# Keys' weight in four pieces between single tiles of x, and a new order for a linear-attention block with an MLP

## The chip, the cores and the metric

The kernel runs on one core of a Trainium2 chip. The time is that of one execution in microseconds of the device, from the chip's own clock; times of a profile are counted from the span's start.

## The reference

`x` is 2048 rows of 512 values in bf16. It is normalised row by row, goes through a linear attention of 32 heads of 16, is normalised again and goes through an MLP with ReLU and 1792 inner values; both parts are added to their input.

```python
h   = x + A(layernorm(x), wqkv, wo)
out = h + B(layernorm(h), w1, w2)

def A(x, wqkv, wo):
    q, k, v = heads(x @ wqkv)
    phi = lambda t: where(t > 0, t + 1, exp(t)) + 1e-6
    pq, pk = phi(q), phi(k)
    kv  = einsum("bhsd,bhse->bhde", pk, v)
    z   = sum of pk over the rows
    num = einsum("bhqd,bhde->bhqe", pq, kv)
    den = einsum("bhqd,bhd->bhq", pq, z) + 1e-6
    return (num / den) @ wo

def B(x, w1, w2):
    return maximum(x @ w1, 0) @ w2
```

## The kernel before

The 2048 rows are 16 tiles of 128 rows (0 to 15), and four chunks of four tiles each. Every instruction is put in its place by hand: `ORDER` is a text of words such as `K.1.3.0.2`, a name and its numbers. The kernel walks through the words and calls `op_<name>` with the numbers. Each engine executes its own instructions in this sequence; semaphores for the data are added automatically. No scheduler moves anything.

The words, by the engine that works on them:

- SyncE's queue (DMAs): `lx.t.n` loads n tiles of x from tile t on (L213); `lk`, `lq`, `lv`, `lo`, `l1`, `l2` load pieces k to k+n of a weight's 128-row blocks (`load_d`, L219); `X.t` and `x.t` transpose a normalised tile by DMA into `lnT` (L293, L294); `wb.c` writes the reciprocal denominators of a chunk to DRAM (L453) and `rb.c.h`, eight of them, read them back spread out into `rr` (L456); `fd.t` writes an output tile (L537). ScalarE's queue has `ax.t.n`, a load of x issued from there (L216).
- VectorE: `S.t` statistics (L233) and `A.t` mean and variance (L234) of a tile; `N.t` its normalised values (L247), by halves with `N.t.k.n`; `M` and `D` the minimum and the sum that finish phi of the keys (L326, L329), `qM`, `qD` of the queries; `dm` the product of queries and `rr` (L469); `hD`, `s`, `a`, `n` the same steps for the second normalisation; `pD` the MLP's ReLU (L513); `fo.t` the output tile (L530). The output tiles have four buffers; tile t uses number t modulo 4.
- ScalarE: `R.t.n` turns variances into 1/sqrt, as a Ln and an Exp (L239, L240); `E.t` copies transposed values from PSUM to `lnT` (L282); `F`, `U` the Exp and the ReLU of the keys (L319, L322), `qF`, `qU` of the queries; `dl4`, `dx4` the reciprocal of the denominators.
- TensorE: `warm` matmuls on zeros (L230); `T.t.b` transposes of a tile into bank b (L272), four of 128x128; `K.t.b` the keys of a tile, four matmuls (L301), by halves with two numbers more; `Q.c.j.b` queries of a chunk (L309); `G.t` the product of normalised x and phi of the keys, summed over all tiles (L353); `z` the sum of the keys (L377), `d4.c` the denominators of a chunk (L425), `kv` (L399) and `m` (L411) the small matrices; `h.t` attention's output (L478); `ph`, `p` the first and `f.t` the second layer of the MLP (L502, L493, L522; an `f` of a tile has 14 matmuls).

Tiles 0 to 4 are transposed by TensorE, tiles 5 to 15 by DMA. Which rows belong to a tile follows from the load words: a load of n tiles gives each partition n rows in a row.

Of the kernel before, what the change touches and what calls it, by code (L numbers as in the profile page):

```python
# [15 lines left out]


ORDER = """
ax.1.1 ax.2.1 table const masks warm.70.7.64 warm.2.7 lx.0.1 S.0 A.0 S.1 lk.0.4 R.0.1 N.0.0.2 lx.3.1 A.1 S.2
R.1.1 lx.4.2 T.0.3.0.2 N.0.2.2 A.2 E.0.0.2 R.2.1 T.0.2.2.2 E.0.2.2 lx.6.2 N.1 lq.0.4 K.0.5.0.2 T.1.3 S.3 lx.8.4  # L20
K.0.5.2.2 N.2 E.1 A.3 R.3.1 lx.12.4 T.2.6 E.2 S.5 N.3 S.4 K.1.0.0.2 A.5 F.0.1 K.1.0.2.2 T.3.3 E.3 K.2.2.0.2
K.2.2.2.2 A.4 S.7 K.3.3.0.2 Q.0.3.1 R.4.2 U.0.1 F.1.1 S.6 F.2.1 N.4 T.4.6 K.3.3.2.2 A.6 A.7 R.6.2 N.5 M.1.1
M.0.1 Q.0.1.5 Q.0.0.4 E.4 U.3.1 S.10 N.6 N.7 M.2.1 D.0.1 A.10 U.1.1 D.1.1 X.5 F.3.1 U.2.1 S.9 S.12 K.4.6 S.8
K.5.7 M.3.1 A.12 A.8 A.9 S.13 S.11 qU.0.0.2 X.6 qF.0.0.2 Q.0.2.0 D.2.1 A.11 K.6.2 A.13 X.7 U.4.2 F.4.2 R.8.2
qM.0.0.2 D.3.1 K.7.3 N.9 M.4.2 N.8 D.4.2 S.14 R.12.2 R.10.2 N.13 A.14 S.15 qF.0.2.2 X.9 N.10 A.15 G.0 G.2 G.1
N.12 G.3 G.4 G.5 X.8 F.6.2 U.6.2 X.13 K.9.3 R.14.2 qU.0.2.2 K.8.2 N.11 M.6.2 qD.0.0.2 D.6.2 N.15 N.14 F.8.2
U.8.2 K.13.1 X.12 X.11 qM.0.2.2 K.12.0 za.4.1 M.8.2 F.12.2 U.12.2 X.10 qD.0.2.2 G.7 K.11.3 X.14 K.10.2 G.6 D.8.2
za.6.0 X.15 K.14.0 F.10.2 M.12.2 lv.2.2 U.10.2 K.15.1 za.8.0 M.10.2 G.9 lv.0.2 zf D.10.2 G.8 zhi D.12.2 F.14.2
G.10 M.14.2 zlo G.12 U.14.2 D.14.2 z.3.3 z.0.3 z.1.3 z.2.3 zc zh G.14 d4.0.3 G.11 G.15 G.13 dl4.0 dx4.0 lo.0.2
gA.0.2 Q.1.1.3 Q.1.0.2 qF.1.0.2 lo.2.2 gD.2.2 kv.1.7 kv.2.7 kv.3.7 kv.0.7 qU.1.0.2 Q.1.3.1 qM.1.0.2 kx qD.1.0.2  # L30
Q.1.2.0 l1.0.2 m.3.7 m.2.6 mD.2.2 wb.0 rb.0.7 rb.0.3 rb.0.0 rb.0.6 rb.0.4 qF.1.2.2 qU.1.2.2 qM.1.2.2 Q.2.1.5
m.1.3 m.0.2 mA.0.2 rb.0.1 rb.0.2 Q.2.0.4 Q.2.3.1 Q.2.2.0 qF.2.0.2 qU.2.0.2 qD.1.2.2 rb.0.5 dm.0.2.2 dm.0.0.2
h.1.6 l1.2.2 d4.1.5 qF.2.2.2 qM.2.0.2 h.0.4 hD.1 dl4.1 s.1 dx4.1 a.1 hD.0 nA.1 s.0 a.0 n.0 Q.3.0.2 l2.0.7 h.2.5
hD.2 s.2 qU.2.2.2 Q.3.1.3 qU.3.0.2 wb.1 x.1 h.3.7 a.2 Q.3.3.6 hD.3 qF.3.0.2 n.2 Q.3.2.5 t.2.0 x.0 ph.0.3.1.0 s.3
a.3 n.3 ph.0.1.3.0 t.3.7 ph.0.0.2.0 rb.1.1 v.2 qM.2.2.2 r.0.4 rb.1.2 rb.1.5 qF.3.2.2 v.3 qM.3.0.2 qM.3.2.2
ph.0.2.0.0 ph.0.2.0.1 rb.1.7 ph.0.3.1.1 qD.2.0.2 qD.3.0.2 ph.0.0.2.1 qU.3.2.2 qD.3.2.2 qD.2.2.2 ph.0.1.3.1
p.0.9.5 p.0.8.4 pA.0.2.2 rb.1.3 rb.1.4 rb.1.6 d4.2.6.2 rb.1.0 dm.1.0.2 l2.7.7 dm.1.2.2 h.4.1 pD.0.0.2 dl4.2
dl4.3 dx4.2 wb.2 rb.2.6 hD.4 s.4 h.5.6 h.7.7 rb.2.7 hD.5 h.6.0 a.4 rb.2.0 rb.2.3 rb.2.4 pA.0.8.2 hD.7 hD.6 s.5
s.6 p.0.7.6 a.5 rb.2.1 p.0.6.5 p.0.4.2 p.0.5.3 s.7 a.6 a.7 p.0.13.1 rb.2.2 rb.2.5 n.4 n.7 n.5 n.6 pD.0.4.2
pD.0.6.2 p.0.11.4 p.0.12.0 dm.2.2.2 dm.2.0.2 dx4.3 p.0.10.3 pD.0.10.2 pD.0.12.2 wb.3 rb.3.4 f.2.6.0.7 rb.3.0  # L40
h.10.5 hD.10 x.6 h.9.4 hD.9 rb.3.2 rb.3.7 h.8.2 s.10 hD.8 a.10 h.11.0 s.9 s.8 rb.3.1 rb.3.6 rb.3.5 rb.3.3 hD.11
a.9 a.8 s.11 n.8 a.11 n.9 f.2.6.7.7 x.7 f.1.7.0.7 f.0.2.0.7 f.0.2.7.7 dm.3.0.2 n.10 n.11 dm.3.2.2 fo.2 fo.0
h.15.3 hD.15 x.5 x.4 x.11 h.12.4 h.13.0 s.15 hD.12 h.14.2 hD.13 a.15 s.12 f.3.3.0.7 x.10 r.4.4 p.1.0.1 hD.14
a.12 s.13 x.9 r.8.4 f.3.3.7.7 s.14 a.13 a.14 p.1.11.6 n.13 n.14 n.15 p.1.10.5 x.8 n.12 fo.3 pD.1.10.2 p.1.1.2
pD.1.0.2 f.1.7.7.7 fd.3 r.12.4 fo.1 p.1.6.3 fd.1 x.14 fd.2 p.1.7.4 p.1.3.1 p.1.4.6 p.1.5.7 p.1.2.0 pD.1.6.2
p.1.13.3 p.1.12.2 pD.1.4.2 pD.1.2.2 x.15 fd.0 x.12 pD.1.12.2 p.2.8.5 p.2.9.6 p.2.6.3 p.2.7.4 p.1.8.1 p.1.9.2
pD.2.8.2 pD.2.6.2 p.2.10.4 p.2.11.5 pD.1.8.2 pD.2.10.2 f.7.6.0.7 f.7.6.7.7 fo.7 p.2.0.4 p.2.1.5 f.4.0.0.7
f.4.0.7.7 x.13 pD.2.0.2 fo.4 f.6.1.0.7 fd.7 f.6.1.7.7 fo.6 f.5.3.0.7 f.5.3.7.7 p.3.4.5 p.3.5.6 fo.5 p.3.11.4
p.3.10.3 p.3.9.1 p.3.8.0 pD.3.4.2 p.3.6.5 p.3.7.6 pD.3.10.2 pD.3.8.2 pD.3.6.2 p.3.0.2 p.3.1.3 pD.3.0.2 p.3.3.1
p.3.2.0 pD.3.2.2 p.3.12.5 p.3.13.6 fd.4 fd.6 p.2.5.3 pD.3.12.2 f.15.4.0.14.3.1 fo.15.3.1 f.15.5.0.14.0.2  # L50
fo.15.0.2 fd.5 p.2.4.2 pD.2.4.2 p.2.3.1 p.2.2.0 p.2.12.6 pD.2.2.2 p.2.13.7 pD.2.12.2 f.8.1.0.7 f.8.1.7.7 fo.8
fd.8 f.12.4.0.7 f.12.4.7.7 fo.12 f.10.7.0.7 f.10.7.7.7 fo.10 f.13.6.0.7 fd.12 fd.10 fd.15.0.2 f.13.6.7.7 fo.13
fd.15.3.1 f.11.0.0.7 f.11.0.7.7 fo.11 fd.13 fd.11 f.14.3.0.7 f.14.3.7.7 fo.14 fd.14 f.9.0.0.7 f.9.0.7.7 fo.9
fd.9 f.15.6.0.14.2.1 fo.15.2.1 fd.15.2.1
"""


# [1 line left out]
def kernel(  # L59
# [157 lines left out]

    def load_d(dst, src, k, n):
        nc.sync.dma_start(out=dst[:, k : k + n, :], in_=src[:, k : k + n, :])  # L219
# [353 lines left out]
```

## Time and profile before

| | |
|---|---|
| median of 3 runs | 169.65 us (169.29 to 170.04) |
| the profiled execution: time / span | 169.61 / 167.9 us |
| granted TensorE clock | 1.00 |
| busy: TensorE / VectorE / ScalarE | 162.2 / 115.8 / 49.9 us |
| read from HBM / written | 9.96 / 2.62 MB |

Busy times are sums of an engine's instructions over the span. A matmul's record begins when its data enter and overlaps its neighbours, so a matmul of 512 columns has a record of 379 ns while the next follows 216 ns later; the chain of waits counts the latter. The profile's SPq and ACTq are the queues of DMA issues of SyncE and ScalarE; an issue's duration there is that of the issuing, and the landing is counted from the issue's start. L numbers are lines of the kernel before.

### The profile page before, as it was taken

Reading aid. Unit: us, or ns where it says so; the run is one execution under the profiler, and the core shown is the slowest. Engines: PE = TensorE matmul, PEld = TensorE weight load, DVE = VectorE, ACT = ScalarE, POOL = GpSimd, SP = SyncE. Lnnn points to the kernel's source line nnn. Section 1 sums busy time; section 2 is a strip of 40 time slices with the busy share of each in tenths; the row PEclk is TensorE's granted clock in tenths of the full one; section 3 lists DMA queues with packets and bytes.
Section 4 is the critical chain, followed back from the end, with each engine's and each line's share of the span. In section 5 each row is a group of like instructions: output and inputs, shape, how many; then the busy total and the mean of one; then the engine's idle time right before and its main releaser. Section 6 shows DMA issues by size and latency. Waiting matters only on the chain.

```text
span 167.9 us, 2399 instructions
## 1 busy us (share of the span) xinstructions
PE 162.2 (97%) x908; PEld 79.5 (47%) x924; DVE 115.8 (69%) x218; ACT 49.9 (30%) x84; POOL 4.7 (3%) x21
## 2 busy tenths in 40 slices
...
GB/s 147 372 234 96 18 106 95 186 315 37 131 341 157 106 228 72 147 43 118 106 94 31 31 89 132 2 0 31 31 66 0 0 0 0 0 66 55 31 62 39
DMA packets 25003, 16.01 MB, mean 95 GB/s; under 512 B 15008, under 2 KB 23968, under 8 KB 24992
## 3 DMA queue, kind: packets, MB, share of 16 engines
...
q8 instruction: 7, 0.11, 0.3%
...
HBM read 9.96 MB, written 2.62 MB: 75 GB/s over the span
## 4 chain that ended last, share of the span: by engine, by line
PE 93%; DVE 2%; DMA 2%; issue 1%
PE bk L522 29%; PE bk L493 26%; PE bk L478 8%; PE bk L301 8%; PE bk L353 8%; PE bk L309 8%; PE bk L502 2%; DMA x_nat<-in_A_x_dram 2%; DVE st L233 1%; PE bk L272 1%; PE bk L425 1%; DVE gT L530 1%; PE bk L377 1%; PE bk L399 1%; PE bk L411 1%
## 5 line engine op out<-in xcount | busy, mean ns | idle before, releaser
L522 PE MATMUL bk<-w_sb,at 128*128 128x512 bf16 (+2 forms) x250 | 49.8, 355 | 0.2
L493 PE MATMUL bk<-lnT,w_sb 128*128 128x512 bf16 x200 | 45.5, 379 | 0.3
L513 DVE TENSOR_SCALAR at<-bk 128x1024 bf16<-128x1024 f32 x26 | 31.4, 1222 | 11.8 <-PE bk L493 9.4
L522 PEld LDWEIGHTS <-at 128*128 128x128 bf16 x252 | 23.6, 98 | 25.4
L493 PEld LDWEIGHTS <-w_sb 128*128 128x128 bf16 x208 | 20.3, 98 | 24.1
L530 DVE SCALAR_TENSOR_TENSOR gT<-bk,rstd,h_nat 128x512 bf16<-128x512 f32 (+2 forms) x18 | 12.4, 691 | 25.5 <-PE bk L522 25.2
L319 ACT ACTIVATE eb<-bk 128x1024 bf16<-128x1024 f32 (+1 forms) x18 | 16.6, 937 | 4.3 <-PE bk L309 1.8
L322 ACT ACTIVATE rb<-bk 128x1024 bf16<-128x1024 f32 (+1 forms) x18 | 16.5, 933 | 0.6 <-PE bk L309 0.6
L301 PE MATMUL bk<-wk_sb,lnT 128*128 128x512 bf16 x62 | 15.4, 380 | 0.1
L309 PE MATMUL bk<-lnT,wq_sb 128*128 128x512 bf16 x62 | 15.3, 379 | 0.1
L478 PE MATMUL bk<-m_sb,pqs 128*128 128x512 bf16 x64 | 15.0, 379 | 0.0
L353 PE MATMUL bk<-at,h_nat 128*128 128x512 bf16 x55 | 13.0, 379 | 0.1
L239 ACT ACTIVATE rstd<-mv,eps 128x2 f32<-128x2 f32 (+2 forms) x14 | 4.2, 298 | 27.1 <-DVE mv L236 24.6
L233 DVE BATCH_NORM_STATS2 st<-x_nat 128x6 f32<-128x512 bf16 x16 | 10.5, 676 | 2.4 <-DMA x_nat<-in_A_x_dram 2.4
L484 DVE TENSOR_TENSOR h_nat<-bk,x_nat 128x512 bf16<-128x512 f32 x16 | 10.7, 679 | 1.0 <-PE bk L478 0.9
L235 DVE BATCH_NORM_STATS2 st<-h_nat 128x6 f32<-128x512 bf16 x16 | 10.6, 680 | 0.2
L478 PEld LDWEIGHTS <-pqs 128*128 128x128 bf16 x64 | 6.1, 98 | 7.8 <-issue 0.7
L309 PEld LDWEIGHTS <-wq_sb 128*128 128x128 bf16 x64 | 6.2, 98 | 7.3
L353 PEld LDWEIGHTS <-h_nat 128*128 128x128 bf16 x64 | 6.1, 98 | 7.3 <-issue 0.2
L301 PEld LDWEIGHTS <-lnT 128*128 128x128 bf16 x64 | 5.8, 98 | 6.8 <-DMA lnT<-h_nat 0.6
L326 DVE TENSOR_SCALAR eb<-eb 128x1024 bf16<-128x1024 bf16 (+1 forms) x18 | 6.8, 388 | 1.6 <-ACT eb L319 1.6
L247 DVE TENSOR_SCALAR h_nat<-x_nat,mv,rstd 128x512 bf16<-128x512 bf16 (+1 forms) x17 | 6.5, 396 | 0.2
...
## 6 DMA issues: line engine op xcount, KB each, us to landing
...
out_dram<-gT SPq DMA_DIRECT2D x15, 128.0 KB, 1.9
...
```

The lines of the kernel that those rows point to most:

```text
L233: op_S = lambda t: nc.vector.bn_stats(out=st[:, t, :], in_=x_nat[:, t, :])
L301: nc.tensor.matmul(bk[:, b, :], lhsT=lnT[c][:, kd, j * P : (j + 1) * P], rhs=wk_sb[:, kd, :], start=(kd == 0), stop=(kd == KD - 1),)
L309: nc.tensor.matmul(bk[:, b, :], lhsT=wq_sb[:, kd, j * P : (j + 1) * P], rhs=lnT[c][:, kd, :], start=(kd == 0), stop=(kd == KD - 1),)
L319: nc.scalar.activation(out=buf(eb, kind, i, n), in_=bank(at_bank[kind, i], n), func=ACT.Exp)
L322: nc.scalar.activation(out=buf(rb, kind, i, n), in_=bank(at_bank[kind, i], n), func=ACT.Relu)
L353: nc.tensor.matmul(bk[:, KD + kd, :], lhsT=ln_nat[:, t, kd * P : (kd + 1) * P], rhs=pk(t)[:, 0, :], start=(not stated), stop=(len(stated) ...
L478: nc.tensor.matmul(bk[:, b, :], lhsT=pqs[:, (c * KD + jb) % NQ, j * P : (j + 1) * P], rhs=m_sb[:, jb, :], start=(jb == 0), stop=(jb == KD ...
L484: nc.vector.tensor_tensor(out=h_nat[:, t : t + n, :], in0=bank(at_bank["h", t], n), in1=x_nat[:, t : t + n, :], op=ALU.add,)
L493: nc.tensor.matmul(bk[:, b, :], lhsT=w1_sb[:, kd, f * P : (f + 1) * P], rhs=lnT[c][:, kd, :], start=(kd == 0), stop=(kd == KD - 1),)
L513: nc.vector.tensor_scalar(out=acts[c % 2][:, f : f + n, :], in0=bank(at_bank["p", c, f], n), scalar1=-1.0, scalar2=0.0, op0=ALU.mult, op1= ...
L522: nc.tensor.matmul(bk[:, b, 0 : w * P], lhsT=acts[c % 2][:, f, j * P : (j + 1) * P], rhs=w2_sb[:, f, k * P : (k + w) * P], start=(f == 0), ...
L530: nc.vector.scalar_tensor_tensor(out=o_t[:, t % NO, cols], in0=bk[:, at_bank["f", t, k], 0 : w * P], scalar=rstd2[:, t : t + 1], in1=h_nat ...
```

## The change

- The keys' weight `wk` (512 KB) comes in four loads of 128 KB, one per 128-row block, between loads of single tiles of x, where it was one load.
- Tiles 1 and 2 are loaded from SyncE's queue, not from ScalarE's; every load is now issued by SyncE.
- Tile 0 is normalised, transposed and copied whole (`N.0`, `T.0.2`, `E.0`), and its keys are one `K.0.6`; they were done in two halves each.
- Tiles 8 to 15 come in one load (`lx.8.8`, 1 MB) instead of two of 4 tiles.
- The rest of `ORDER` is laid out anew, with other banks and another sequence; the set of matmuls is the same. A new function `op_ak` (a load of `wk` from ScalarE's queue) is defined and not used.

The diff, cut to the head of the order and the places that the prediction speaks of:

```diff
 ORDER = """
-ax.1.1 ax.2.1 table const masks warm.70.7.64 warm.2.7 lx.0.1 S.0 A.0 S.1 lk.0.4 R.0.1 N.0.0.2 lx.3.1 A.1 S.2
-R.1.1 lx.4.2 T.0.3.0.2 N.0.2.2 A.2 E.0.0.2 R.2.1 T.0.2.2.2 E.0.2.2 lx.6.2 N.1 lq.0.4 K.0.5.0.2 T.1.3 S.3 lx.8.4
-K.0.5.2.2 N.2 E.1 A.3 R.3.1 lx.12.4 T.2.6 E.2 S.5 N.3 S.4 K.1.0.0.2 A.5 F.0.1 K.1.0.2.2 T.3.3 E.3 K.2.2.0.2
-K.2.2.2.2 A.4 S.7 K.3.3.0.2 Q.0.3.1 R.4.2 U.0.1 F.1.1 S.6 F.2.1 N.4 T.4.6 K.3.3.2.2 A.6 A.7 R.6.2 N.5 M.1.1
...
-G.10 M.14.2 zlo G.12 U.14.2 D.14.2 z.3.3 z.0.3 z.1.3 z.2.3 zc zh G.14 d4.0.3 G.11 G.15 G.13 dl4.0 dx4.0 lo.0.2
-gA.0.2 Q.1.1.3 Q.1.0.2 qF.1.0.2 lo.2.2 gD.2.2 kv.1.7 kv.2.7 kv.3.7 kv.0.7 qU.1.0.2 Q.1.3.1 qM.1.0.2 kx qD.1.0.2
...
+table const masks warm.70.7.64 warm.2.7 lx.0.1 S.0 lx.1.1 lx.2.1 A.0 R.0.1 S.1 A.1 N.0 lk.0.1 S.2 lk.1.1 lk.2.1
+T.0.2 R.1.1 lx.3.1 N.1 T.1.7 E.0 A.2 lk.3.1 R.2.1 S.3 K.0.6 N.2 T.2.2 A.3 E.1 K.1.3.0.2 K.1.3.2.2 lx.4.2 S.5
+R.3.1 N.3 S.4 A.5 E.2 F.0.1 T.3.4 E.3 A.4 lx.6.2 S.7 S.6 K.2.7.0.2 K.2.7.2.2 lq.0.4 R.4.2 N.4 K.3.0.0.2 Q.0.3.1
+N.5 A.7 U.0.1 A.6 F.1.1 U.1.1 T.4.2 R.6.2 M.1.1 K.3.0.2.2 E.4 U.2.1 Q.0.0.3 M.0.1 U.3.1 D.1.1 lx.8.8 N.6 N.7
+D.0.1 X.5 Q.0.1.4 S.12 S.9 S.8 A.12 A.9 A.8 F.3.1 M.3.1 S.10 S.13 S.11 X.6 A.13 D.3.1 qF.0.0.2 qU.0.0.2 K.4.5
...
+K.14.0 K.15.1 za.8.0 zf F.14.2 lo.0.2 U.14.2 D.12.2 lo.2.2 M.10.2 G.9 l1.0.2 Q.1.1.3 zhi D.10.2 zlo M.14.2 G.11
+G.10 D.14.2 z.0.0 z.2.0 z.3.0 z.1.0 G.14 zc zh d4.0.0 dl4.0 dx4.0 wb.0 rb.0.2 G.13 rb.0.5 G.12 G.15 gA.2.2
...
+qD.1.2.2 dm.0.0.2 Q.2.2.0 Q.2.3.1 dm.0.2.2 h.1.2 qF.2.0.2 qU.2.0.2 l1.2.2 qM.2.0.2 qU.2.2.2 hD.1 d4.1.4 dl4.1
...
+p.0.11.7 dm.1.0.2 dm.1.2.2 h.6.1 pD.0.10.2 dl4.2 dx4.2 ph.0.0.2.1 hD.6 h.5.4 l2.7.7 pD.0.0.2 wb.2 rb.2.4 hD.5
...
+fo.12 fd.12 fd.13 fd.10 f.8.6.0.7 f.8.6.7.7 fo.8 fd.8 f.15.5.0.14.3.1 fo.15.3.1 fd.15.3.1
 """
...
+    def op_ak(k, n):
+        nc.scalar.dma_start(out=wk_sb[:, k : k + n, :], in_=wqkv_v[:, k : k + n, D : 2 * D])
+
     op_lk = lambda k, n: load_d(wk_sb, wqkv_v[:, :, D : 2 * D], k, n)
```

More of the change, by code (lines that the diff above doesn't have):

```diff
@@ L18 @@
 ORDER = """
-ax.1.1 ax.2.1 table const masks warm.70.7.64 warm.2.7 lx.0.1 S.0 A.0 S.1 lk.0.4 R.0.1 N.0.0.2 lx.3.1 A.1 S.2
-R.1.1 lx.4.2 T.0.3.0.2 N.0.2.2 A.2 E.0.0.2 R.2.1 T.0.2.2.2 E.0.2.2 lx.6.2 N.1 lq.0.4 K.0.5.0.2 T.1.3 S.3 lx.8.4
-K.0.5.2.2 N.2 E.1 A.3 R.3.1 lx.12.4 T.2.6 E.2 S.5 N.3 S.4 K.1.0.0.2 A.5 F.0.1 K.1.0.2.2 T.3.3 E.3 K.2.2.0.2
-K.2.2.2.2 A.4 S.7 K.3.3.0.2 Q.0.3.1 R.4.2 U.0.1 F.1.1 S.6 F.2.1 N.4 T.4.6 K.3.3.2.2 A.6 A.7 R.6.2 N.5 M.1.1
-M.0.1 Q.0.1.5 Q.0.0.4 E.4 U.3.1 S.10 N.6 N.7 M.2.1 D.0.1 A.10 U.1.1 D.1.1 X.5 F.3.1 U.2.1 S.9 S.12 K.4.6 S.8
@@ L24 @@
[L24 to L28, printed above, removed]
@@ L29 @@
-G.10 M.14.2 zlo G.12 U.14.2 D.14.2 z.3.3 z.0.3 z.1.3 z.2.3 zc zh G.14 d4.0.3 G.11 G.15 G.13 dl4.0 dx4.0 lo.0.2
-gA.0.2 Q.1.1.3 Q.1.0.2 qF.1.0.2 lo.2.2 gD.2.2 kv.1.7 kv.2.7 kv.3.7 kv.0.7 qU.1.0.2 Q.1.3.1 qM.1.0.2 kx qD.1.0.2
-Q.1.2.0 l1.0.2 m.3.7 m.2.6 mD.2.2 wb.0 rb.0.7 rb.0.3 rb.0.0 rb.0.6 rb.0.4 qF.1.2.2 qU.1.2.2 qM.1.2.2 Q.2.1.5
-m.1.3 m.0.2 mA.0.2 rb.0.1 rb.0.2 Q.2.0.4 Q.2.3.1 Q.2.2.0 qF.2.0.2 qU.2.0.2 qD.1.2.2 rb.0.5 dm.0.2.2 dm.0.0.2
-h.1.6 l1.2.2 d4.1.5 qF.2.2.2 qM.2.0.2 h.0.4 hD.1 dl4.1 s.1 dx4.1 a.1 hD.0 nA.1 s.0 a.0 n.0 Q.3.0.2 l2.0.7 h.2.5
@@ L34 @@
[L34 to L53, printed above, removed]
@@ L54 @@
-fd.9 f.15.6.0.14.2.1 fo.15.2.1 fd.15.2.1
+table const masks warm.70.7.64 warm.2.7 lx.0.1 S.0 lx.1.1 lx.2.1 A.0 R.0.1 S.1 A.1 N.0 lk.0.1 S.2 lk.1.1 lk.2.1
[3 more added lines that the diff above has]
+D.0.1 X.5 Q.0.1.4 S.12 S.9 S.8 A.12 A.9 A.8 F.3.1 M.3.1 S.10 S.13 S.11 X.6 A.13 D.3.1 qF.0.0.2 qU.0.0.2 K.4.5
@@ new lines @@
+K.5.6 X.7 F.4.2 A.11 A.10 Q.0.2.0 K.6.2 U.4.2 F.2.1 S.14 M.4.2 R.8.2 R.10.2 R.12.2 K.7.3 M.2.1 N.9 X.9 A.14 G.0
+G.3 D.2.1 N.8 F.6.2 qF.0.2.2 U.6.2 N.11 D.4.2 S.15 N.13 A.15 R.14.2 N.12 M.6.2 G.1 G.2 qM.0.2.2 qU.0.2.2 N.10
+D.6.2 qM.0.0.2 G.4 G.5 K.9.3 X.8 K.8.2 N.14 X.13 G.6 K.13.1 X.12 X.11 qD.0.0.2 N.15 X.10 K.12.0 G.7 za.4.1 F.8.2
+U.8.2 M.8.2 qD.0.2.2 X.14 X.15 D.8.2 F.12.2 U.12.2 K.11.3 K.10.2 G.8 za.6.0 lv.2.2 lv.0.2 F.10.2 M.12.2 U.10.2
+K.14.0 K.15.1 za.8.0 zf F.14.2 lo.0.2 U.14.2 D.12.2 lo.2.2 M.10.2 G.9 l1.0.2 Q.1.1.3 zhi D.10.2 zlo M.14.2 G.11
```

21 lines of the change are left out of this document (added).

## The prediction

> **What bounds the kernel now.** I read the profile's page first: which engine is full, and whose work makes up the chain that ended last.
>
> ```profile
> PE 162.2 (97%) x908; PEld 79.5 (47%) x924; DVE 115.8 (69%) x218; ACT 49.9 (30%) x84; POOL 4.7 (3%) x21
> ...
> PE 93%; DVE 2%; DMA 2%; issue 1%
> ```
>
> TensorE is busy 97% of the span and is 93% of the chain. The change adds and removes no matmul (both orders hold the same ones, only in another sequence), so it can move the end only where TensorE waits. The chain of waits in order of time tells where that is:
>
> ```profile
> 0.79 2.80 DMA x_nat<-in_A_x_dram
> ...
> 6.61 0.29 PE bk L272 x2
> 6.89 0.43 PE bk L301 x2
> ...
> 9.28 0.23 PE bk L272 x4
> 9.50 1.30 PE bk L301 x6
> ...
> 37.57 0.33 PE bk L425 x4
> ...
> 49.26 0.86 PE bk L478 x4
> ...
> 164.12 0.76 DVE gT L530
> ```
>
> Up to 6.61 us the chain is the load of tile 0, its statistics and its normalisation. From there it is TensorE without a hole up to the last output at 164.12, apart from pieces of 0.05 called issue. So there is nothing to win after 6.9 us, only something to lose; what there is to win lies in the head. My mark is the moment at which the transposes of tiles 0 to 3 and the key matmuls of tiles 0 and 1 are done: 9.50 now. The same work precedes K.2 in the new order, so a shift of this mark is a shift of the end, as long as no new hole opens behind it.
>
> **The head, step by step.** VectorE, ScalarE and TensorE between the first landing and the mark:
>
> ```profile
> 3.62 0.69 DVE L233 BATCH_NORM_STATS2 st<-x_nat 128x6 f32<-128x512 bf16 x1 [2.38 <-DMA x_nat<-in_A_x_dram]
> 4.34 0.18 DVE L234 BATCH_NORM_AGGREGATE mv<-st 128x2 f32<-128x6 f32 x1
> 4.44 0.66 DVE L233 BATCH_NORM_STATS2 st<-x_nat 128x6 f32<-128x512 bf16 x1
> ...
> 6.47 0.17 DVE L234 BATCH_NORM_AGGREGATE mv<-st 128x2 f32<-128x6 f32 x1
> 6.56 0.38 DVE L247 TENSOR_SCALAR h_nat<-x_nat,mv,rstd 128x512 bf16<-128x512 bf16 x1
> 6.85 0.69 DVE L233 BATCH_NORM_STATS2 st<-x_nat 128x6 f32<-128x512 bf16 x1
> 7.46 0.40 DVE L247 TENSOR_SCALAR h_nat<-x_nat,mv,rstd 128x512 bf16<-128x512 bf16 x1
> ...
> 8.63 0.41 DVE L247 TENSOR_SCALAR h_nat<-x_nat,mv,rstd 128x512 bf16<-128x512 bf16 x1
> ```
>
> ```profile
> 4.56 0.29 ACT L239 ACTIVATE rstd<-mv,eps 128x1 f32<-128x1 f32 x1 [1.56 <-DVE mv L234]
> 4.89 0.20 ACT L240 ACTIVATE rstd<-rstd 128x1 f32<-128x1 f32 x1
> ...
> 8.40 0.20 ACT L240 ACTIVATE rstd<-rstd 128x1 f32<-128x1 f32 x1
> 8.51 0.58 ACT L282 ACTIVATE lnT<-bk 128x512 bf16<-128x512 bf16 x1
> ```
>
> ```profile
> 9.11 0.39 PE L272 MATMUL bk<-ident,h_nat 128*128 128x128 bf16 x4
> ```
>
> Differences of these starts are the steps I use. S to the next instruction 0.61 (6.85 to 7.46); S to its own A 0.72; A to the next 0.09 to 0.10; N to the next 0.30 (6.56 to 6.85). A to ScalarE's Ln 0.22; Ln to Exp 0.33; Exp to the N that waits for it 0.23 (8.40 to 8.63); Exp to the next on ScalarE 0.11. N to its transposes 0.48 (8.63 to 9.11); transposes to the copy E 0.40; E to K 0.64 (0.58, and 0.06 from end to start). Four transposes take 0.22 on the chain (9.28), a K of four matmuls 0.86 (six took 1.30 from 9.50).
>
> *VectorE in the new order* (S0 A0 S1 A1 N0 S2 N1 A2 S3 N2 A3 S5 N3), with tile 0 at 3.62 as now: A0 4.34, S1 4.44, A1 5.16, N0 5.25, S2 5.55, N1 6.16, A2 6.46, S3 6.55. R2's Ln at 6.68 and Exp at 7.01 let N2 go at 7.24; A3 7.54, S5 7.63. R3's Ln 7.76, Exp 8.09: N3 at 8.32, where it is 8.63 now. The gain comes from tile 0 being normalised in one instruction, not two with a wait each, and from A1 standing ahead of N0.
>
> *TensorE*: T.0 at 5.25 + 0.48 = 5.73, E.0 at 6.13 (R1's Exp, at 5.71, is past), so K.0 could start at 6.77; T.1 stands ahead of it (6.16 + 0.48 = 6.64 to 6.86), so K.0 runs 6.86 to 7.72. T.2 7.72 to 7.94, K.1 to 8.80, T.3 (8.32 + 0.48 = 8.80) to 9.02. E.2 follows R3's Exp at 8.20 and ends at 8.78, in time for K.2 at 9.02. The mark moves from 9.50 to 9.02: **0.48 us earlier**.
>
> *The loads that this needs.* SyncE now issues all of them:
>
> ```profile
> 1.25 0.41 SPq L219 DMA_DIRECT2D wk_sb<-in_A_wqkv_dram  x1
> 1.72 1.45 SPq L213 DMA_DIRECT2D x_nat<-in_A_x_dram  x3
> ```
>
> ```profile
> x_nat<-in_A_x_dram SPq DMA_DIRECT2D x2, 128.0 KB, 3.6
> ```
>
> ```profile
> 4.00:4.50 0.50, 0.50 (x13) 0.50 (x11) 0.47 (x3) 0.00 (x0) 0.38 (x3) 1.00 1.09 356
> 10.00:11.00 1.00, 1.00 (x6) 0.41 (x5) 1.00 (x3) 0.97 (x5) 0.00 (x0) 1.00 0.83 320
> 11.00:12.00 1.00, 1.00 (x10) 0.57 (x8) 1.00 (x7) 1.00 (x4) 0.00 (x0) 1.00 0.04 16
> ```
>
> Issues follow each other by 0.47 (1.25 to 1.72). From 0.79 on: tiles 0, 1, 2 at 0.79, 1.26, 1.73; keys' weight, three quarters, at 2.20, 2.67, 3.14; tile 3 at 3.61; the last quarter at 4.08; tiles 4 and 5 at 4.55, 6 and 7 at 5.02, lq 5.49, tiles 8 to 15 at 5.96. From issue to landing a single tile took 2.8 (tile 0, from the chain) when nothing was queued ahead of it, and 4.4 as tile 3, with the 512 KB of the weight ahead (the row's 3.6 is the median of these two). One 131,000-byte load per 0.47 us is 279 GB/s, under the 356 GB/s that the queue moved at 4.0 to 4.5, so no backlog should build up in front of the singles, and I take the end 2.8. Tile 1 is then there at 4.06 (needed 4.44), tile 2 at 4.53 (5.55), tile 3 at 6.41 (6.55), the last quarter at 6.88 (its matmul, the fourth of K.0, starts at 7.51), tiles 4 and 5 with a second tile's 0.37 (131,000 bytes at 356 GB/s) at 7.7 (7.63, which N3's wait for R3 hides). The large load: the transfers are over at 11.0 now (320 GB/s to there, 16 after); the singles run behind full rate by at most 8 x (0.47 - 0.37) = 0.8, so tile 15 is in by about 12.4. VectorE reaches S.12, counted on from N3 in the same steps (four S, four A, four N, two M and two D stand between), at about 13.
>
> A rule of the Trainium skill speaks against the small loads: "DMA: Bandwidth & Descriptors", section "Bandwidth", advises batching to 1 MiB or more for three quarters of the peak rate, and lists 138 GB/s for a transfer of 64 KB and 341 for one of 1 MB. By an estimate from those figures, at the page's 138 GB/s each, eight singles in a row would take 7.6 us and miss the times above; the trace's 356 GB/s with singles and halves in flight speaks for overlap, and no run here shows eight singles in a row yet.
>
> *ScalarE's queue* gives up two issues of 0.4 us before its table load; it is idle until 4.56 anyway, so that is worth nothing. The four waits of K.0, in place of one, are for events that are past by the sum above: nothing, or the lateness of the last quarter.
>
> **Behind the head.** All else that the new order does is worth nothing if it opens no hole. I went along the distances in TensorE work between each producer and its consumer. K.4 to G.5 stand at the same amount of TensorE work as before, so the filler matmuls keep their cover, with the DMA transposes of tiles 5 to 7 released 0.4 us earlier by N.5. The one distance that shrinks and leads through DMAs is from d4.0 to h.1, because Q.1.1 moved ahead of z:
>
> ```profile
> 39.33 0.34 SPq L453 DMA_DIRECT2D scr<-rd  x1
> 41.07 3.61 SPq L456 DMA_DIRECT2D rr<-scr  x8
> ```
>
> ```profile
> 47.69 0.69 DVE L469 TENSOR_TENSOR pqs<-pqT,rr 128x1024 bf16<-128x1024 bf16 x1
> ```
>
> Now h.1 starts 49.26 - 37.90 = 11.36 after d4.0's end; without one Q (0.86) that is 10.50, and its third matmul, which needs the second dm, is at 10.93. The first dm starts now at 47.69, that is 9.79 after d4.0's end; two of them take 1.3, so at the latest that gives 11.1 and a hole of 0.2. The last of the eight broadcasts is issued near 44.2; with a load's 2.8 it lands 9.1 after d4.0, the dms end at 10.4, and no hole opens. I take none, and keep 0.2 as an end. The second chunk is alike: h.6 comes 0.6 sooner after h.1 than h.4 did, behind the same wb, rb, dm; another 0 to 0.3. At the tail, fo.8 reuses the output buffer of fo.12, the tile just before it: one f of 14 matmuls (3.0 us) must cover fo.12 (0.76), an issue and a landing. It does up to 2.2 us of landing.
>
> **Sum.** The profiled execution took 169.61 us, 1.7 around its span of 167.9; the median of the runs shown is 169.65, so they are the same. 169.61 - 0.48 = 169.13, to which nothing is added: **169.1 us**.
>
> **Rivals.**
> *A, the gain is eaten later.* The holes at h.1 (0.2), at h.6 (0.3) or a similar one at a tile's DMA transpose in the first chunk take 0.2 to 0.6 back: 169.3 to 169.7. For it: no distance there has more than a few tenths of slack, and a new order means new tight places. Against it: the old order, made with the same instruction lengths, shows not one hole of that kind in 157 us.
> *B, the singles land late, and the kernel is slower.* If the seventh and eighth loads take 4.4 from issue, as tile 3 does now, tile 3 lands at 8.01, not 6.41. S.3 stands ahead of N2 and A3 on VectorE: S3 8.01, N2 8.62, A3 8.92, R3's Exp 9.47, N3 9.70, T.3 at 10.18 to 10.40, the mark at 10.40: 0.9 late, 170.5; with 0.50 per issue, 170.8. It decides from tile 3 landing past 7.0 (3.4 after issue), where the gain is gone. For it: 4.4 is a measured value for just this tile. Against it: then 0.9 MB was queued in the first 1.3 us of issuing, now it comes in at 279 GB/s. The skill's batching rule (same page and section) points the same way.
> *C, a larger gain.* Tile 0 is alone at the start, where it now shares the DMA engines with tile 1 from ScalarE's queue. If it lands 0.4 sooner and the others keep pace with their issues, VectorE runs 0.3 to 0.4 ahead of my times: 168.7.
>
> **Chances.** Forecast (169.0 to 169.3) 0.47, A 0.23, B and holes of its size 0.21, C 0.09. A measurement of this kernel can tell about 0.5% (0.85 us) from no change: faster means under 168.8, slower over 170.5. C gives faster 0.1; forecast and A are within; of B some lies within, and larger holes than I found are put to slower: 0.2. The range reaches from C's 168.7 to B's upper 170.8.
>
> **What would show it.** Right: S.3 without a wait for its load; the fourth matmul of K.0 right behind the third; N.3 near 8.3, T.3 ending near 9.0; then a chain of TensorE work alone up to the output. Wrong: VectorE idle before S.3 or S.5 released by a DMA, TensorE waiting at K.0's fourth matmul for wk (B); an idle time on TensorE's weight loads released by pqs L469 or a DMA into lnT around 48 to 62 us (A); the last fo of tile 8 released by a DMA out instead of by TensorE. A chain with several new holes in the middle that I haven't named would make the whole forecast wrong.

## The result, and the profile after

The changed kernel takes **170.94 us** (median of 14 runs, 169.93 to 172.23) beside 169.76 (169.29 to 171.74) for the kernel before on the same chip: ratio **1.0066 [1.0045, 1.0087]**. I had said 169.1 in 168.7 to 170.8: it became slower where I forecast a little faster, and the time lies above the range. The profiled execution took 171.28 us with a span of 169.6, where it was 169.61 with 167.9: 1.7 us to account for. In the kernel after (and in most experiments) a line has a number by one or two lower or higher than before: S is L235, N L249, T L274, K L303, the loads of x L212, those of weights L218, h L480. The granted clock is 1.00 as before.

First the page, its busy times and the chain by engine:

```profile
PE 162.6 (96%) x907; PEld 79.8 (47%) x924; DVE 114.6 (68%) x216; ACT 50.6 (30%) x84; POOL 4.7 (3%) x21
...
PE 91%; DMA 3%; SPq 2%; issue 1%; DVE 0%
```

TensorE does the same work (162.6 us, before 162.2) in a longer span, and 3% of the chain is now DMA. VectorE from its first statistics on (start, duration, what, and in brackets the idle time before it and its releaser):

```profile
2.82 0.69 DVE L235 BATCH_NORM_STATS2 st<-x_nat 128x6 f32<-128x512 bf16 x1 [1.57 <-DMA x_nat<-in_A_x_dram]
...
4.44 0.48 DVE L249 TENSOR_SCALAR h_nat<-x_nat,mv,rstd 128x512 bf16<-128x512 bf16 x1
...
6.38 0.69 DVE L235 BATCH_NORM_STATS2 st<-x_nat 128x6 f32<-128x512 bf16 x1 [0.34 <-DMA x_nat<-in_A_x_dram]
7.33 0.41 DVE L249 TENSOR_SCALAR h_nat<-x_nat,mv,rstd 128x512 bf16<-128x512 bf16 x1 [0.26 <-ACT rstd L242]
7.66 0.17 DVE L236 BATCH_NORM_AGGREGATE mv<-st 128x2 f32<-128x6 f32 x1
9.15 0.69 DVE L235 BATCH_NORM_STATS2 st<-x_nat 128x6 f32<-128x512 bf16 x1 [1.32 <-DMA x_nat<-in_A_x_dram]
9.76 0.40 DVE L249 TENSOR_SCALAR h_nat<-x_nat,mv,rstd 128x512 bf16<-128x512 bf16 x1
```

Tile 0 is there 0.8 us earlier than before (2.82, not 3.62), and N.0 runs at 4.44. Then the lead melts: S.3 waits 0.34 for tile 3, and S.5 stands 1.32 us in front of N.3 on VectorE, waiting for tiles 4 and 5. N.3, due at 8.32, starts at 9.76. TensorE and the chain of waits from that load on:

```profile
10.22 0.40 PE L274 MATMUL bk<-ident,h_nat 128*128 128x128 bf16 x4 [1.16 <-DVE h_nat L249]
```

```profile
4.56 4.57 DMA x_nat<-in_A_x_dram
9.13 0.02 issue
9.15 0.04 DVE st L235
9.19 0.57 issue
9.76 0.41 DVE h_nat L249
10.17 0.05 issue
10.22 0.40 PE bk L274 x4
10.61 1.29 PE bk L303 x6
```

My mark is at 10.61 where it was 9.50: **1.11 us late**, forecast was 0.48 early. From there on TensorE works through, and h.1 starts at 50.29 (before 49.26: still 1.03 late). The last piece of the chain, VectorE's last output, stands at 166.41 (before 164.91: 1.50). So some 0.5 more is lost behind h.1. TensorE's matmuls, and the weight loads of h.6 (L480), show two places:

```profile
57.47 0.61 PE L274 MATMUL bk<-ident,hn 128*128 128x128 bf16 x8
58.20 1.03 PE L504 MATMUL bk<-lnT,w_sb 128*128 128x256 bf16 x8
...
62.76 1.04 PE L495 MATMUL bk<-lnT,w_sb 128*128 128x512 bf16 x4
63.65 1.21 PE L480 MATMUL bk<-m_sb,pqs 128*128 128x512 bf16 x4
```

```profile
63.65 0.11 PEld L480 LDWEIGHTS <-pqs 128*128 128x128 bf16 x2 [0.34 <-DVE pqs L471]
64.25 0.11 PEld L480 LDWEIGHTS <-pqs 128*128 128x128 bf16 x2 [0.49 <-DVE pqs L471]
```

Eight transposes, one every 0.06, start at 57.47, and the first matmul of the MLP (`ph`, L504) only at 58.20: 0.3 lost. The four matmuls of h.6, the first of the second chunk, take 1.21 where the four before them take 1.04: 0.2 lost, waiting for dm, the hole of rival A. (The weight loads' own idle times are longer; most of that lies beside running matmuls.) The remaining 0.2 of the 1.7 lie behind VectorE's last output.

Why are tiles 4 and 5 late? The DMA issues of SyncE's queue, after:

```profile
0.80 1.34 SPq L212 DMA_DIRECT2D x_nat<-in_A_x_dram  x3
2.19 1.38 SPq L218 DMA_DIRECT2D wk_sb<-in_A_wqkv_dram  x3
3.61 0.43 SPq L212 DMA_DIRECT2D x_nat<-in_A_x_dram  x1
4.08 0.43 SPq L218 DMA_DIRECT2D wk_sb<-in_A_wqkv_dram  x1
4.56 0.91 SPq L212 DMA_DIRECT2D x_nat<-in_A_x_dram  x2
5.51 0.43 SPq L218 DMA_DIRECT2D wq_sb<-in_A_wqkv_dram  x1
5.99 0.50 SPq L212 DMA_DIRECT2D x_nat<-in_A_x_dram  x1
```

The issues come exactly when I said. Tiles 4 and 5 land at 9.13, that is 4.57 after theirs; I had given them 3.2. Before, they were issued at 2.25, took 5.3 and were in at 7.6. What the DMA engines moved, first before, then after, from 4.0 to 7.5 us (the last two columns are their busy share and GB/s):

```profile
4.00:7.50 3.50, 2.70 (x29) 1.60 (x27) 3.44 (x11) 2.03 (x8) 1.80 (x7) 1.00 1.07 373
```

```profile
4.00:7.50 3.50, 3.02 (x31) 2.14 (x30) 2.86 (x8) 1.94 (x8) 1.81 (x7) 1.00 0.84 234
```

From 1.5 to 4.0 both moved the same (217 and 215 GB/s). After 4.0 the kernel before has everything up to tile 15 issued by 4.7 and runs at 373; the changed one runs at 234, and is 139 GB/s x 3.5 us = 0.49 MB behind at 7.5. At 373 that is 1.3 us, which is about the lateness of tiles 4 and 5 against the forecast (9.13 and 7.7).

### The profile page after: what moved, and what is told of

Same layout as the page of the kernel before. It is cut to its first block, busy times and chain, and to the rows that moved or that the text cites. A ratio compares the mean times of both kernels' runs of the same rounds, so it can differ in the third digit from the quotient of the medians.

```text
span 169.6 us, 2394 instructions
## 1 busy us (share of the span) xinstructions
PE 162.6 (96%) x907; PEld 79.8 (47%) x924; DVE 114.6 (68%) x216; ACT 50.6 (30%) x84; POOL 4.7 (3%) x21
## 4 chain that ended last, share of the span: by engine, by line
PE 91%; DMA 3%; SPq 2%; issue 1%; DVE 0%
PE bk L524 28%; PE bk L495 26%; PE bk L480 8%; PE bk L355 8%; PE bk L311 8%; PE bk L303 7%; DMA x_nat<-in_A_x_dram 3%; PE bk L504 2%; SPq L218 1%; SPq L212 1%; PE bk L427 1%; PE bk L274 1%; PE bk L379 1%; PE bk L401 1%; PE bk L413 1%
## 5 line engine op out<-in xcount | busy, mean ns | idle before, releaser
L524 PE MATMUL bk<-w_sb,at 128*128 128x512 bf16 (+2 forms) x248 | 49.3, 355 | 0.2
L495 PE MATMUL bk<-lnT,w_sb 128*128 128x512 bf16 x201 | 46.0, 379 | 0.4
L515 DVE TENSOR_SCALAR at<-bk 128x1024 bf16<-128x1024 f32 x26 | 31.4, 1222 | 11.1 <-PE bk L495 10.2
L532 DVE SCALAR_TENSOR_TENSOR gT<-bk,rstd,h_nat 128x512 bf16<-128x512 f32 (+2 forms) x18 | 12.4, 691 | 27.0 <-PE bk L524 27.0
L303 PE MATMUL bk<-wk_sb,lnT 128*128 128x512 bf16 x62 | 15.2, 379 | 0.3 <-ACT lnT L284 0.3
L480 PE MATMUL bk<-m_sb,pqs 128*128 128x512 bf16 x64 | 15.3, 380 | 0.0
L235 DVE BATCH_NORM_STATS2 st<-x_nat 128x6 f32<-128x512 bf16 x16 | 10.5, 680 | 3.2 <-DMA x_nat<-in_A_x_dram 3.2
L480 PEld LDWEIGHTS <-pqs 128*128 128x128 bf16 x64 | 6.0, 98 | 7.7 <-DVE pqs L471 1.1
L303 PEld LDWEIGHTS <-lnT 128*128 128x128 bf16 x64 | 6.0, 98 | 7.2 <-ACT lnT L284 0.8
L249 DVE TENSOR_SCALAR h_nat<-x_nat,mv,rstd 128x512 bf16<-128x512 bf16 x16 | 6.4, 413 | 0.3 <-ACT rstd L242 0.3
```

Source lines behind the costliest of these rows:

```text
L235: op_S = lambda t: nc.vector.bn_stats(out=st[:, t, :], in_=x_nat[:, t, :])
L303: nc.tensor.matmul(bk[:, b, :], lhsT=lnT[c][:, kd, j * P : (j + 1) * P], rhs=wk_sb[:, kd, :], start=(kd == 0), stop=(kd == KD - 1),)
L480: nc.tensor.matmul(bk[:, b, :], lhsT=pqs[:, (c * KD + jb) % NQ, j * P : (j + 1) * P], rhs=m_sb[:, jb, :], start=(jb == 0), stop=(jb == KD ...
L495: nc.tensor.matmul(bk[:, b, :], lhsT=w1_sb[:, kd, f * P : (f + 1) * P], rhs=lnT[c][:, kd, :], start=(kd == 0), stop=(kd == KD - 1),)
L515: nc.vector.tensor_scalar(out=acts[c % 2][:, f : f + n, :], in0=bank(at_bank["p", c, f], n), scalar1=-1.0, scalar2=0.0, op0=ALU.mult, op1= ...
L524: nc.tensor.matmul(bk[:, b, 0 : w * P], lhsT=acts[c % 2][:, f, j * P : (j + 1) * P], rhs=w2_sb[:, f, k * P : (k + w) * P], start=(f == 0), ...
```

## The experiments

My theory after this reading: the loads cost some 1.1 us in the head, and the new order some 0.4 at h.6. The rival to it: the new order itself (S.5 ahead of N.3, tighter distances) costs the time, with the old loads as well. Ratios are against the kernel before on the same chip.

### Loads and order apart

The new order with the old loads:

```diff
-table const masks ... lx.0.1 S.0 lx.1.1 lx.2.1 A.0 R.0.1 S.1 A.1 N.0 lk.0.1 S.2 lk.1.1 lk.2.1 T.0.2 ... lx.8.8
+ax.1.1 ax.2.1 table const masks ... lx.0.1 S.0 A.0 R.0.1 S.1 A.1 N.0 lk.0.4 S.2 T.0.2 ... lx.8.4 lx.12.4
```

> The new order of compute with the loads of the kernel before: tiles 1 and 2 from ScalarE's queue, the keys' weight in one load, tiles 8 to 15 in two. Theory L (the loss in the head is the late landing of tiles 4 and 5, in front of which S.5 and so N.3 stand; a smaller rest is a hole before h.6): S.5 without a wait, N.3 at 8.3 to 8.6, T.3 ends at 9.0 to 9.3 (10.61 with the new loads), the hole before h.6 of 0.3 to 0.5 stays, so 169.6 to 170.0. Theory O (the new order loses by itself behind the head, and the head's lateness would be made up): 170.5 or more.

Measured: 169.78, **0.9992 [0.9975, 1.0009]**: no difference from the kernel before, within the range of theory L.

And the new loads in the old order (`lx.1.1`, `lx.2.1`, four `lk` and `lx.8.8` in SyncE's queue, the rest as before):

> The old order of compute with the new loads: all from SyncE's queue, singles of tiles 0 to 3, the keys' weight in four pieces between them, tiles 8 to 15 in one load. Theory L: S.5 stands ahead of N.3 in the old order too, so tiles 4 and 5 landing near 9.1 put N.3 at 9.7 and the mark at 10.6, 1.1 late, and no hole later: 170.6 to 170.9. Theory O: within 0.3 us of the kernel before.

Measured: 172.2, **1.0152 [1.0121, 1.0182]**. That is beyond the 170.6 to 170.9 that I expected. VectorE waits for x five times, 5.7 us in all, 1.7 of it for tile 0 (statistics are L232 here, the keys' matmuls L300, the queries' L308):

```profile
DVE st L232 <- DMA x_nat<-in_A_x_dram: 5.7, 5, 1.8
...
PEld L300 <- DMA lnT<-h_nat: 2.6, 5, 1.5
PEld L308 <- DMA wq_sb<-in_A_wqkv_dram: 1.9, 1, 1.9
```

So the loads are what costs. The new order is the better one for them: with it they cost 0.66%, in the old one 1.5%.

### S.5 behind N.3

If the place of S.5 on VectorE is what turns a late load into a late TensorE, moving it helps:

```diff
-lx.4.2 S.5 R.3.1 N.3 S.4 A.5
+lx.4.2 R.3.1 N.3 S.5 S.4 A.5
```

> The changed kernel with one word moved: S.5 behind N.3 on VectorE. Theory L: N.3 no longer waits for tiles 4 and 5 and runs at 8.3 to 8.5, T.3 ends near 9.1; the late landing is met again at T.4 (S.5 at 9.1, N.4 about 11.2, T.4 at 11.7 where TensorE would come at 11.2), so 0.8 to 1.0 of the 1.1 us comes back: 169.9 to 170.2. Theory O: no change from 170.9.

Measured: 170.88, **1.007 [1.0048, 1.0092]**: nothing gained; my expectation missed. The wait does go, and N.3 runs at 8.21, close to the 8.32 of my sum. But the next loads are late too:

```profile
8.21 0.41 DVE L249 TENSOR_SCALAR h_nat<-x_nat,mv,rstd 128x512 bf16<-128x512 bf16 x1 [0.60 <-ACT rstd L242]
...
15.24 1.88 DVE L235 BATCH_NORM_STATS2 st<-x_nat 128x6 f32<-128x512 bf16 x3 [1.31 <-DMA x_nat<-in_A_x_dram]
```

```profile
11.25 1.04 PE L311 MATMUL bk<-lnT,wq_sb 128*128 128x512 bf16 x4 [0.88 <-DMA wq_sb<-in_A_wqkv_dram]
```

Queries' weight holds TensorE for 0.88 and tiles 8 to 15 hold VectorE at S.12 for 1.31. It is not one load in an awkward place: all that is issued behind the pieces is late.

### Keys' weight in one load, in two, in four

Everything as changed, but `wk` whole in the place of its first piece:

```diff
-N.0 lk.0.1 S.2 lk.1.1 lk.2.1 T.0.2 R.1.1 lx.3.1 N.1 T.1.7 E.0 A.2 lk.3.1 R.2.1
+N.0 lk.0.4 S.2 T.0.2 R.1.1 lx.3.1 N.1 T.1.7 E.0 A.2 R.2.1
```

> The changed kernel with the keys' weight in one 512 KB load at the place of its first quarter; all loads still from SyncE's queue. Theory L with the cause in the small loads (twelve issues, the transfer engines not kept busy between them): tiles 4 and 5 are issued at 3.1 instead of 4.6 and land at 7.5 to 7.9, N.3 at 8.3 to 8.6: 169.7 to 170.1. Theory L with the cause in the one queue or the 1 MB load: landing still past 8.5, 170.5 or more. Theory O: no change from 170.9.

Measured: 169.72, **1.0005 [0.9991, 1.0019]**. Its issues, and VectorE at S.3, S.5 and N.3:

```profile
2.18 0.43 SPq L218 DMA_DIRECT2D wk_sb<-in_A_wqkv_dram  x1
2.66 1.45 SPq L212 DMA_DIRECT2D x_nat<-in_A_x_dram  x3
4.15 0.43 SPq L218 DMA_DIRECT2D wq_sb<-in_A_wqkv_dram  x1
4.63 0.50 SPq L212 DMA_DIRECT2D x_nat<-in_A_x_dram  x1
```

```profile
6.90 0.69 DVE L235 BATCH_NORM_STATS2 st<-x_nat 128x6 f32<-128x512 bf16 x1 [0.87 <-DMA x_nat<-in_A_x_dram]
...
7.91 0.66 DVE L235 BATCH_NORM_STATS2 st<-x_nat 128x6 f32<-128x512 bf16 x1
8.60 0.41 DVE L249 TENSOR_SCALAR h_nat<-x_nat,mv,rstd 128x512 bf16<-128x512 bf16 x1
```

Tiles 4 and 5 are now issued at 3.2 and land at 7.6, and S.5, the row at 7.91, waits for nothing. Tile 3, with 512 KB just ahead, lands at 6.88 and costs 0.87: that eats the gain that tile 0 had made, and no more. In two loads of 256 KB:

> The changed kernel with the keys' weight in two loads of 256 KB, at the places of the first and the last quarter: two issues fewer than with four. L1: the later loads are issued 0.9 us earlier; tiles 4 and 5 land near 8.0, tiles 8 to 15 near 13.3; about a third of the 1.2 us is left, 169.8 to 170.2. L2: in the middle, 170.2 to 170.5.

Measured: 170.48, **1.0045 [1.0016, 1.0074]**. L1 stands for the cost of the issues, L2 for small pieces that run badly in themselves (both are spelled out with the next run); the time lies in L2's range, not in L1's, though tiles 4 and 5 land at 8.2, as L1 had it. One, two and four loads give 1.0005, 1.0045 and 1.0066: each more costs, though the steps between two and four lie within the intervals.

### The pieces in ScalarE's queue

The unused `op_ak` put to use: four pieces of `wk` from ScalarE's queue, the tiles from SyncE's.

> The changed kernel with the four pieces of the keys' weight issued by ScalarE behind its table load, beside SyncE's loads of x (four singles, then 4+5, 6+7, lq, 8 to 15). If the loss is that four pieces take three more issues of 0.47 us in front of all later loads in one queue (theory L1): tiles 4 and 5 are issued at 2.7 and land by 7.6, N.3 near 8.3 to 8.6, 169.5 to 169.9. If it is the small pieces themselves that keep the transfer engines from their rate (theory L2): landing still past 8.5, 170.4 or more.

Measured: 170.17, **1.0029 [0.9995, 1.0062]**, between the ranges of L1 and L2. With the pieces out of its queue SyncE issues tiles 4 and 5 at 2.7 and they land at 6.7; T.3 starts at 8.84, the earliest yet beside the run with S.5 moved. But `lq` and tiles 8 to 15 are issued no sooner than 5.56 and 6.0, and S.12 waits 1.03 for tiles 8 to 15. SyncE's own waits name the reason:

```profile
SPq L218 <- DMA x_nat<-in_A_x_dram: 1.2, 1, 1.2
SPq L212 <- DMA x_nat<-in_A_x_dram: 0.9, 1, 0.9
```

The issue of `lq` (L218) stands from 4.4 to 5.56 until a load of x has landed, and tile 2 lands at 5.55. The data don't ask for this: `lq` writes a buffer of its own. In the trace it waits for the semaphore that told of tile 2's landing, and then uses the same one. Each load from the ninth on, counted over both queues, does so with the semaphore of an earlier load; in the changed kernel these had all landed by then, and SyncE shows no such wait.

Inconclusive as a kernel. For the question it says two things. Freed of the pieces, the same loads of x are issued 1.9 us sooner and land 2.4 us sooner. And loads of 128 KB are not slow in themselves. From 2.5 to 3.5 us, when almost all that was under way were loads of this size, the DMA engines moved, first in the changed kernel, then here:

```profile
2.50:3.50 1.00, 1.00 (x24) 1.00 (x21) 0.68 (x1) 0.00 (x0) 0.81 (x4) 1.00 0.84 240
2.50:3.50 1.00, 1.00 (x24) 1.00 (x22) 0.04 (x1) 0.00 (x0) 0.81 (x4) 1.00 1.07 365
```

Issued by two queues, they run at 365 GB/s; by one, at 240. That speaks for the issues (L1) and against the pieces themselves (L2).

### The large load

> The changed kernel with tiles 8 to 15 in two loads of 512 KB instead of one of 1 MB. L1 and L2: the landing of tiles 4 and 5 (9.1) and of lq (11.1) stays, the mark stays at 10.6; tiles 8 to 11 land near 12.8 instead of 14.6, so VectorE's second wait goes: 170.5 to 171.0. If the 1 MB load takes the transfer engines from the loads ahead of it: tiles 4 and 5 land by 8.2 and 169.9 or less.

Measured: 171.11, **1.0081 [1.0051, 1.011]**: two loads of 512 KB in place of the 1 MB load give nothing back. Tiles 4 and 5 happened to land at 7.8 in this run, but 6 and 7 (wait 0.77), `lq` (TensorE waits 1.67) and tiles 12 to 15 (S.12 waits 0.65) were late instead. Which load is late is not fixed: in the five profiles whose loads up to `lq` are issued at the same moments (the changed kernel, the new loads in the old order, S.5 moved, this one and the next), tiles 4 and 5 landed between 7.8 and 9.1, tiles 6 and 7 between 9.5 and 11.2, and `lq` between 10.8 and 12.5. The rate from 4.0 to 7.5 was low in all five, 230 to 258 GB/s.

### The hole at h.6

The changed kernel's head word for word up to `K.8.2`, then the old order:

> The changed kernel's head and loads word for word up to K.8.2, and from there the kernel before's order. Theory (two costs: about 1.1 us from late loads in the head, about 0.4 us from the shorter distance between the first chunk's denominators and h.6): the hole in front of h.6 goes (no wait of TensorE for pqs of 0.5 or more between 55 and 66 us), the late loads stay, so 0.3 to 0.6 us less than the changed kernel: 170.3 to 170.6, ratio 1.004. Rival (the loads are all of it and the hole only takes up slack that the end would lose elsewhere): 170.9, ratio 1.0066 as the changed kernel.

Measured: 170.78, **1.0047 [1.0022, 1.0071]**. In its profile h.1 is 1.48 late (50.74), and the last output 1.47 (166.38): no loss behind h.1. The same head with the weight in one load:

> Keys' weight in one load in its first piece's place, the new head, and the kernel before's order behind K.8.2. Theory of two costs: the weight in one load took back 1.1 us (169.72), and the h.6 hole's 0.4 goes with the old rest: 169.1 to 169.4, ratio 0.997, the first version below the kernel before. Rival (hole not a cost of its own): 169.7, ratio 1.000.

Measured: 169.63, **0.9978 [0.995, 1.0006]**. Here h.1 is 0.10 late and the end 0.09. The two profiles with the new order and good loads show the opposite: with the weight in one load h.1 is 0.12 early and the end 0.45 late, with the old loads 0.07 early and 0.39 late. The other runs say the same. In all nine profiles with the new rest the end is later than h.1 is, by 0.25 to 0.67, and in all five with the old rest both are shifted alike, to 0.01. So the profiles show the loss behind h.1 (at h.6 and at `ph` together) wherever the new rest is, and only there. The medians lean the same way, 1.0066 to 1.0047 and 1.0005 to 0.9978, but these intervals overlap, and with the old loads the new order came out level. The loss is shown in the profiles; its size in the median, 0 to 0.4 us, is not settled.

With the large load in two halves again:

> As the run with the weight in one load and the old rest, but tiles 8 to 15 in two loads of 512 KB as before. Theory (the large load's late landing costs only where S.12 or S.8 waits; with the weight in one load tiles 8 to 15 were in by 12.9, when VectorE got there): no difference within 0.2 us, 169.1 to 169.5. Rival (a 1 MB load lands late in some runs and makes the spread): 0.3 less than with one load and a spread as narrow as the kernel before's.

Measured: 169.67, **0.9996 [0.9968, 1.0024]**: no difference that can be told, as expected, though the time is above the 169.1 to 169.5 that I gave.

One more version put tile 3 ahead of the one load of `wk`, with 60 instead of 70 warm-up matmuls and the old rest:

> A version put together from what the runs showed: the new order up to K.8, then the old order; loads all on SyncE, tile 3 ahead of the keys' weight, which is one load; 60 warm-up matmuls of 64 columns instead of 70, so that T.0 isn't held until 5.6. T.0 at 5.1, S.3 without a wait, tiles 4 and 5 land at 7.6, N.3 at 8.2, the mark at 8.9 (9.50 in the kernel before), no hole before h.6: 168.9 to 169.2. If the first chunk's holes come from the head's shift and not from the new order, they stay and it is 169.4 or more.

Measured: 170.28, **1.0026 [1.0002, 1.005]**, far above what I gave. The profiled execution was the fastest of its twelve, 169.16 with T.3 at 8.81, about as expected; the others reach to 172.48. The order of issues that looks best in one profile is not the best in the median. No profile of the others was taken. All that is known of them is the granted clock, 0.99 on average in the two longest (171.36 and 172.48) and 0.998 to 1.00 in the rest; what else differs stays open.

### Three issues that carry nothing

What was still open: do the pieces cost by the three more issues, or by how transfers of 128 KB run? The weight in one load, and three loads of 4 KB in the places of the other pieces:

```diff
-N.0 lk.0.1 S.2 lk.1.1 lk.2.1 T.0.2 R.1.1 lx.3.1 N.1 T.1.7 E.0 A.2 lk.3.1 R.2.1
+N.0 lk.0.4 S.2 li li T.0.2 R.1.1 lx.3.1 N.1 T.1.7 E.0 A.2 li R.2.1
...
+    def op_li():
+        nc.sync.dma_start(out=hn[0:16, 3, 0:P], in_=wqkv_v[0:16, 0, 0:P])
```

> Keys' weight in one load as in the run with one load (169.72), and in the places of the other three pieces three loads of 4 KB each (16 rows of 256 bytes) that nothing uses: the same twelve issues of SyncE's queue as in the changed kernel, at the same moments, but hardly a byte in the three. Theory (the pieces cost by the queue's 0.47 us per issue: the loads behind are issued 1.4 us later and land about 4.5 to 5 after that): tiles 4 and 5 are issued at 4.55 and land near 9, S.5 waits over 1 us, 170.6 to 171.0, ratio 1.005 to 1.0066. Rival (the transfers of 128 KB themselves run badly, and what is issued later into an emptier queue lands sooner after its issue): tiles 4 and 5 land by 8.0 (3.4 after issue), ratio 1.0005 to 1.002, 169.7 to 170.0.

Measured: 176.04, **1.0326 [1.0281, 1.037]**. This failed as an experiment: all three write the same place, so each waits for the one before, and SyncE's queue with it.

```profile
2.66 4.34 DMA hn<-in_A_wqkv_dram
...
7.02 1.57 DMA hn<-in_A_wqkv_dram
```

Tile 3, behind them, is issued at 7.38. With a place of its own for each (`hn[0:16, i, 0:P]`):

> As the run before, but the three 4 KB loads go to three different places, so that none waits for another (to one place, each waited for the one before to land, and SyncE's queue stood until 8.6 us: 176.0). Theory (the queue's 0.47 us per issue): tiles 4 and 5 are issued at 4.55 and land near 9, S.5 waits over 1 us, 170.6 to 171.0, ratio 1.005 to 1.0066. Rival (the 128 KB transfers themselves): tiles 4 and 5 land by 8.0, ratio 1.0005 to 1.002, 169.7 to 170.0.

Measured: 170.83, **1.0054 [1.0028, 1.008]**. Twelve kilobytes in three issues cost in the median about what the pieces do, where the same kernel without them is level (1.0005 [0.9991, 1.0019]). VectorE in that run, at S.3, S.5 and S.12 (statistics are L238):

```profile
7.47 0.69 DVE L238 BATCH_NORM_STATS2 st<-x_nat 128x6 f32<-128x512 bf16 x1 [1.43 <-DMA x_nat<-in_A_x_dram]
...
8.48 0.66 DVE L238 BATCH_NORM_STATS2 st<-x_nat 128x6 f32<-128x512 bf16 x1
...
14.38 1.88 DVE L238 BATCH_NORM_STATS2 st<-x_nat 128x6 f32<-128x512 bf16 x3 [0.32 <-DMA x_nat<-in_A_x_dram]
```

Right in the time, not in the place: not S.5 but S.3 waits (tile 3, issued 1.0 later than with the weight alone, lands 0.6 later), and then S.12. Tiles 4 and 5 land at 8.12, 3.5 after their issue: that is close to the rival's sign (by 8.0, 3.4 after issue) and not near 9. And in the head the empty issues do only about half of what the pieces do. T.3 starts at 9.63; it was 9.07 with the weight in one load and 10.22 in the changed kernel. From 1.5 to 7.5 us the DMA engines moved 244 GB/s, with the weight in one load 263, in the changed kernel 226. So three more issues are enough for a loss of this size in the median. That they are all of what the pieces cost is not shown; the other half of the lateness in the head stays open.

## Why the prediction was wrong

- **What bounds the kernel: right.** TensorE without a hole, what can be won lies in the head. Nothing was won or lost between the mark and h.1 in the changed kernel (1.11 and 1.03).
- **The steps on VectorE and TensorE: right.** With S.5 out of the way N.3 came at 8.21 (forecast 8.32). Tile 0 was even 0.8 earlier than I counted, the beginning of rival C; but T.0 and T.1 ran from 5.61 only, behind warm-up matmuls that end at 5.39, and that lead was lost on the waits behind.
- **The issues: right**, to 0.03 us for each of the twelve.
- **The landings: the step that failed.** "No backlog should build up in front of the singles", and tiles 4 and 5 at 7.7 as 2.8 and a second tile's 0.37 after their issue. The singles themselves bore it out, or nearly: 2.0 to 2.2 for tiles 0 to 2, 2.7 for tile 3 (at 6.3, forecast 6.41), 2.2 to 3.2 for the pieces. The two-tile load took 4.6 and not 3.2, tiles 6 and 7 landed at 9.8, `lq` at 11.1, tiles 8 to 15 at 14.6, not "by about 12.4". I had compared the singles' 279 GB/s with a peak of 356 and called the difference slack. It is the reverse: while one queue issues singles, it hands the DMA engines no more than 279 GB/s. They moved 234 from 4.0 to 7.5, less still than the issuing explains, and the 0.49 MB that they didn't move then is missing for every load behind. The kernel before's own trace had a value for just this load, 5.3 us from issue to landing (2.25 to 7.6, with much queued ahead); I gave it 3.2 from the singles. I had allowed "at most 8 x (0.47 - 0.37) = 0.8" for this at tile 15 alone, took it as hidden, and gave tiles 4 and 5, which come right behind, none of it.
- **Rival B had the size and the sign, not the place.** It let tile 3 be late past 7.0 and put the time at 170.5 to 170.8; tile 3 came at 6.3, and the next load stood on the path in its place, with S.5 ahead of N.3. The question for B should have been which of all loads has the least slack: in my own numbers that was tiles 4 and 5, 7.7 against 7.63.
- **Rival A's hole at h.6 opened**, 0.2 us in the profile, inside the 0 to 0.3 that I kept as an end and took at nothing. With it came 0.3 in front of `ph`, a place that I hadn't named. At h.1 none opened, and at the tail fo.8 had its cover, both as planned.
- **The Trainium skill's rule** in "DMA: Bandwidth & Descriptors", section "Bandwidth", on batching to 1 MiB spoke against the change, and the sign of the time agrees. My estimate from its figures, 7.6 us for eight singles, is near the 6.5 that they took (0.80 to 7.3), but not for its reason: it lets them run one after the other, and here they overlapped, each taking 2.0 to 3.2 from issue to landing. The same page's section "Issuing engines are not separate DMA queues" calls the time to initiate a DMA "usually small relative to the DMA itself". For one load the runs agree: 0.47 us of issue beside 2.0 to landing. For a row of them they don't: an issue takes 0.47 us, the data of a single tile 0.37 at 356 GB/s, and three issues with hardly a byte cost 0.5%.

No version beat the kernel before beyond doubt; the weight in one load with the old rest comes nearest (0.9978 [0.995, 1.0006]).
